# New durations in the planner that orders an attention stage, on one core

## The chip, the cores and the metric

The kernel runs on one core of a Trainium2 chip. The metric is the device time of one execution in microseconds; the time before is 968.0, the median of three runs (967.85 to 968.37). The engines are TensorE (PE for its matmuls, PEld for its weight loads), VectorE (DVE), ScalarE (ACT), GpSimd (POOL) and SyncE (SP, which only issues DMAs here). TensorE writes into PSUM, eight banks of 128 x 512 floats; the other engines read the banks, and a bank can take its next matmul only after its reader is done.

## The reference

For x of 2048 rows and 448 columns the kernel computes a gated mix of two branches, all in float32:

```python
g = sigmoid((x * gate_w).sum(-1, keepdims=True))
qkv = x @ wqkv                        # 16 heads of 28
scores = q @ k.T * 28 ** -0.5         # per head, 2048 x 2048
a = (softmax(scores) @ v) @ wo
b = (gelu(x @ w_gate) * (x @ w_up)) @ w_down    # 1792 hidden columns
out = g * a + (1 - g) * b
```

## The kernel before, in words

It has three stages. The first computes q, k and v from x. The last, behind attention, multiplies the hidden activations with w_down and the attention's output with wo. The middle one is attention, and TensorE's free slots in it are filled with the products x @ w_up and x @ w_gate. The change touches only the order of this middle stage.

Precision: each float32 operand is split into a high and a low part, so that a score tile takes three matmuls of a group (`product`), and a block of the hidden layer 42 (`cross`).

TensorE's array is used as four groups of 32 rows. A score needs only 28 rows plus two for a shift, and x and the weights of the hidden layer are laid out in pieces of 32 rows. So four matmuls, one for each row group, run side by side. The code calls this a step. In each step every group r does one matmul: either one of the three of its current score (`("score", ...)`, line 174), or one of its current hidden block (`("cross", ...)`, line 183). A group that has neither, or has no bank for a new block, has an empty slot in that step.

Attention goes in 32 turns: 16 heads, and for each head two halves of its keys (8 key tiles of 128 by 4 query tiles of 512: 32 score tiles). At a turn's end the value matmuls (`values`, 64 of them over the full array) sum the turn's exponentials into one bank, and DVE takes it out (`add`).

A score tile leaves its bank in one of two ways. Either ACT takes the exponential straight from the bank into SBUF (`exponential`, line 780), or DVE copies it to SBUF (`aside`, line 784) and ACT takes the exponential in place later. A finished hidden block is copied out by DVE (`clear`, line 797) and stored by SP. The eight banks serve all of this: up to four hidden blocks in progress, up to two scores in progress, and what waits for its reader.

The order of it all is written out before the kernel is built, by the function `plan` (lines 75 to 286). It is a small clockwork with its own time `s.now` for TensorE, `s.act`, `s.dve` and `s.sp` for the other queues, `s.bank[b]` for the moment at which bank b may be used again, and `s.tiles` for the exponentials' buffers. The constants at the top of the file are its durations in nanoseconds:

- STEP, the time of a step; READ and SEEN, from a score's end to the moment at which ACT and DVE may begin with it;
- EXP, what an exponential occupies ACT for, EXP_OUT, its time until the result is out; COPY, what a copy occupies DVE for and, before the change, also its time until the result is out;
- BACK, from a reader's end to the bank's next use;
- VALUES, INTO, OUTOF, the value matmuls of one key tile, the passage into them and out of them;
- ISSUE and LAND, SP's time for a DMA and a DMA's time to land.

`run` starts a score in some group as soon as a bank is free by this clock, at most two at a time. `step` advances all groups, and starts a new hidden block only when a bank is free. `end_score` decides between exponential and copy by which would be out first. `values` waits by the clock until the turn's exponentials are done. For each turn 25 preferences among the groups are tried, and the four states that promise the earliest end are carried on; the best at the end gives the list of operations.

The kernel then issues exactly this list. On the chip no time of the planner counts any more: each instruction waits for its semaphores, in the order of its engine's queue. What the planner's clock does is to choose the order, the bank of each block, and which tiles are copied.

Of the kernel before, what the change touches and what calls it, by code (L numbers as in the profile page):

```python
# [37 lines left out]

TURN, LEAD, NPT, FIRST = 8, 4, 36, 4
OFFSET = (0, 6, 21, 27)  # L40
STEP, READ, SEEN = 227, 270, 200
ISSUE, LAND = 520, 5000
EXP, EXP_OUT, COPY, BACK = 480, 620, 690, 100
VALUES, INTO, OUTOF = 857, 90, 203
EARLY = 7
HOLES = (0, 1, 2, 3)
XLOADS = (6, 9, 11, 14, 16, 19, 21, 24)
# [2 lines left out]
SLIP, LATE, AHEAD = 200, 12, 6  # L50
# [8 lines left out]
def piece(n):  # L59

    return n // 21 * 2 + (n % 21 >= 12)
# [13 lines left out]
def plan(blocks):  # L75
# [10 lines left out]

    def begin():
        s = State()
        s.now = s.act = s.dve = s.sp = s.turn = 0
        s.pos, s.next, s.since = list(OFFSET), [0] * 4, [0] * 4  # L90
        s.bank, s.tiles, s.where, s.seen = [0] * 8, [-n for n in range(NPT)], {}, {}
        s.score, s.mine = [None] * 4, [None] * 4
        s.late, s.waiting, s.arrive, s.stores = [], [], [], []
        s.parted = s.loaded = 6
        s.fetch = None
        s.ops, s.past = [], None
        return s

    def take(s):
        b = s.bank.index(min(s.bank))  # L100
        s.bank[b] = NEVER
        return b

    def next_tile(s, key):
        holes = HOLES if turn_of[key] == len(turns) - 1 else ()
        return min((t, n) for n, t in enumerate(s.tiles) if n not in holes)

    def hold(s, key):
        t, n = next_tile(s, key)
        s.where[key], s.tiles[n] = n, NEVER  # L110
        return t

    def run_act(s, key, src, ready):
        if src is not None:
            ready = max(ready, hold(s, key))
        t = max(s.act, ready)
        s.act = t + EXP
        s.seen[key] = t + EXP_OUT + BACK
        s.ops.append(("exp", key, s.where[key], src))
        if src is not None:  # L120
            s.bank[src] = s.seen[key]

    def run_late(s, until):
        s.late.sort(key=lambda a: (turn_of[a[1]], a[0]))
        while s.late and max(s.act, s.late[0][0]) <= until:
            ready, key = s.late.pop(0)
            run_act(s, key, None, ready)

    def run_dve(s, ready):
        s.dve = max(s.dve, ready) + COPY  # L130
        return s.dve + BACK

    def end_score(s, r):
        key, b, _ = s.score[r]
        s.score[r] = None
        run_late(s, s.now + READ - SLIP)
        tile = next_tile(s, key)[0]
        if s.waiting or tile == NEVER:
            s.waiting.append((key, b, s.now + READ))
            return  # L140
        direct = max(s.act, s.now + READ, tile) + EXP_OUT
        copied = max(s.dve, s.now + SEEN, tile) + COPY
        if copied - (0 if turn_of[key] == s.turn else SLIP) < direct and len(s.late) < LATE:
            s.bank[b] = run_dve(s, max(s.now + SEEN, hold(s, key)))
            s.ops.append(("copy", key, s.where[key], b))
            s.late.append((s.bank[b], key))
        else:
            run_act(s, key, b, s.now + READ)

    def fetch(s):  # L150
        if s.fetch is not None:
            run_sp(s, s.now, (5 if s.fetch % 2 else 8) if s.fetch < len(turns) - 2 else 0)
            s.ops.append(("fetch", s.fetch))
            s.fetch = None

    def run_sp(s, ready, n):
        s.sp = max(s.sp, ready) + ISSUE * n

    def store(s, until):
        while s.stores and s.stores[0][0] <= until:  # L160
            ready, *what = s.stores.pop(0)
            run_sp(s, ready, 1)
            s.ops.append(("store", *what))

    def can_cross(s, r):
        return s.pos[r] < end and piece(s.pos[r]) < s.parted

    def step(s):
        did = []
        for r in range(4):  # L170
            if s.score[r]:
                key, b, n = s.score[r]
                s.ops.append(("score", r, key, n, b))
                s.score[r][2] += 1
                did.append((r, True))
            elif can_cross(s, r) and (s.mine[r] is not None or min(s.bank) <= s.now):
                first = s.mine[r] is None
                if first:
                    s.mine[r] = take(s)
                n = s.pos[r]  # L180
                s.pos[r] += 1
                s.ops.append(("cross", r, n, s.mine[r], first, (n + 1) % 42 == 0 or n + 1 == goal[r]))
                did.append((r, False))
        s.now += STEP
        for r, scored in did:
            n = s.pos[r]
            if scored and s.score[r][2] == 3:
                end_score(s, r)
            if not scored and n < end and (n % 42 == 0 or n == goal[r]):
                b, s.mine[r] = s.mine[r], None  # L190
                s.bank[b] = run_dve(s, s.now + SEEN)
                s.ops.append(("clear", r, n - 1, b))
                s.stores.append((s.bank[b], r, n - 1))
                if n == goal[r]:
                    s.pos[r] = last
        while s.loaded < 2 * blocks + 8 and piece(min(s.pos)) >= s.loaded - 5:
            s.ops.append(("load", s.loaded))
            s.loaded += 1
            run_sp(s, s.now, 4)
            s.arrive.append(s.sp + LAND)  # L200
            fetch(s)
        store(s, s.now)
        while s.arrive and s.arrive[0] <= s.now:
            s.arrive.pop(0)
            s.parted += 1

    def run(s, n, todo, first, liking):
        want = sum(todo)
        done = k = 0
        while k < n or any(todo) or any(s.score):  # L210
            while done < want and k >= first and min(s.bank) <= s.now and sum(map(bool, s.score)) < 2:
                can = [r for r in range(4) if todo[r] and not s.score[r]]
                if not can:
                    break
                r = max(can, key=lambda r: (s.mine[r] is None, not 0 < -s.pos[r] % 42 <= 2, todo[r] + liking[r],
                                            s.now - s.since[r]))
                need = sum(not s.score[q] and (can_cross(s, q) if s.mine[q] is None else 0 < -s.pos[q] % 42 <= 2)
                           for q in range(4))
                if s.mine[r] is not None and (sum(b <= s.now for b in s.bank) <= need or done * n >= want * (k + AHEAD)):
                    break  # L220
                s.since[r] = s.now
                s.score[r] = [items[r][s.next[r]], take(s), 0]
                s.next[r] += 1
                todo[r] -= 1
                done += 1
            step(s)
            k += 1

    def values(s, i):
        store(s, NEVER)  # L230
        fetch(s)
        h, k0 = turns[i]
        keys = [(kt, (h, kt, q)) for kt in range(k0, k0 + TURN) for q in range(4)]
        while any(turn_of[key] == i for _, key in s.late):
            ready, key = s.late.pop(0)
            run_act(s, key, None, ready)
        s.now = max(s.now, min(s.bank), *(s.seen.pop(key) - VALUES * (kt - k0) for kt, key in keys))
        b = take(s)
        s.now += INTO
        s.ops.append(("values", i, b))  # L240
        for kt, key in keys:
            s.tiles[s.where.pop(key)] = s.now + VALUES * (kt - k0 + 1) + BACK
        while s.waiting:
            run_act(s, *s.waiting.pop(0))
        s.now += TURN * VALUES
        run_late(s, s.now + OUTOF)
        s.bank[b] = run_dve(s, s.now + SEEN) if i < len(turns) - 1 else NEVER
        s.now += OUTOF
        s.ops.append(("sum", i))

    def left(s):
        return sum(end - p if p >= last else g - p + 42 for g, p in zip(goal, s.pos))

    best = [begin()]
    for i, _ in enumerate(turns):
        tried = {}
        for old in best:
            for liking in [(0,) * 4, *permutations(range(4))]:
                for cut in CUTS if i == len(turns) - 1 else (0,):
                    s = old.copy()  # L260
# [15 lines left out]
    for s in best:  # L276
        while min(s.pos) < end:
            step(s)
        store(s, NEVER)
    s = min(best, key=lambda s: s.now)  # L280
    kept, free = s.mine, sorted((t, b) for b, t in enumerate(s.bank) if b not in s.mine)
    ops = []
    while s:
        ops = s.ops + ops
        s = s.past
# [778 lines left out]
```

## Time and profile before

| what | us |
|---|---|
| median of three runs | 968.0 |
| profiled execution | 967.61 |
| its span, first to last instruction | 965.8 |
| TensorE busy with matmuls | 959.8 |
| ACT busy | 658.3 |
| DVE busy | 564.4 |
| POOL busy | 416.1 |

In the views below a row of a group gives line, engine, operation, output<-input, shape and count, then busy time, mean duration in ns, and the idle time of that engine before it with what ended it. A row of one tile's view gives the durations as minimum, median and maximum in ns, and where in the span the first and the last lie. A row of the timeline gives the start and the duration in us; where several instructions are merged (x2, x3) the duration is from the first's start to the last's end. A row of windows gives the stretch, its length, TensorE's busy time with the count of its matmuls, the granted clock, the DMA share and GB/s. `b<-Q,wk` is a score's matmul, `b<-X,wk` one of the hidden layer, `b<-pt,VH` a value matmul, `pt<-b` an exponential or a copy out of a bank, `pt<-pt` an exponential in place, `u<-b` a hidden block's copy.

### The profile page before, as it was taken

What the parts mean: (1) busy time and instruction counts of PE and PEld (TensorE: products, weight loads), DVE (VectorE), ACT (ScalarE), POOL (GpSimd) and SP (SyncE); (2) the same over time, 40 slices, a digit from 0 to 9 for tenths busy, and PEclk for the clock granted to TensorE, in tenths of its full rate; (3) what the DMA queues carried; (4) which work ended last, traced back from release to release, by engine and by line L of the source; (5) the groups of instructions that cost most, each with busy time, mean ns of one, the idle gap of its engine ahead of it and who ended that gap; (6) DMA issues with size and microseconds to landing.
All of it is one profiled execution on the core that took longest, in us unless ns stands there. A gap on an engine that the chain in (4) does not pass through costs nothing.

```text
span 965.8 us, 27893 instructions
## 1 busy us (share of the span) xinstructions
PE 959.8 (99%) x11192; PEld 737.8 (76%) x11192; DVE 564.4 (58%) x873; ACT 658.3 (68%) x1260; POOL 416.1 (43%) x614
## 2 busy tenths in 40 slices
PE   9999999999999999999999999999999999999998
PEld 7878977666777776677777666777766679999997
DVE  6572366555656655566566555666655578765743
ACT  4332588776888778777788877788887797553530
POOL 6426553464646546554545655563564111210000
PEclk9999999999999999999999999999999999999999
DMA  7687786766667777666767775665776949967612
GB/s 237 205 269 225 249 223 169 216 182 181 189 192 194 203 190 197 177 172 194 196 176 217 209 204 147 202 183 170 216 197 186 288 138 343 328 215 250 202 60 77
DMA packets 108376, 194.83 MB, mean 202 GB/s; under 512 B 30716, under 2 KB 46108, under 8 KB 108244
## 3 DMA queue, kind: packets, MB, share of 16 engines
q1 hardware_dynamic: 92548, 160.98, 55.8%
q0 software_dynamic: 14864, 31.26, 11.3%
q8 instruction: 88, 1.44, 0.7%
q10 hardware_dynamic: 832, 0.79, 0.3%
q14 instruction: 44, 0.36, 0.1%
HBM read 131.99 MB, written 60.95 MB: 200 GB/s over the span
## 4 chain that ended last, share of the span: by engine, by line
PE 94%; DMA 3%; POOL 2%; issue 1%; SPq 0%; ACT 0%; DVE 0%; DVEq 0%; POOLq 0%; ACTq 0%
PE b L296 86%; PE pqk L296 7%; DMA vd<-V 1%; POOL wsd L302 1%; DMA VH<-vd 0%; DMA raw<-in_xT 0%; POOL whl L306 0%; DMA wsd<-whl 0%; DMA wraw<-in_wu 0%; DMA wk<-wsd 0%; POOL wk L302 0%; POOL whl L305 0%; SPq L299 0%; POOL wk L306 0%; POOL wk L305 0%
## 5 line engine op out<-in xcount | busy, mean ns | idle before, releaser
L296 PE MATMUL b<-X,wk 32*128 32x512 f32 x4704 | 459.9, 387 | 0.0
L296 PE MATMUL b<-Q,wk 32*128 32x512 f32 x3072 | 445.5, 390 | 0.0
L296 PEld LDWEIGHTS b<-X,wk 32*128 32x128 f32 x4704 | 407.2, 183 | 18.0 <-issue 12.0
L780 ACT ACTIVATE pt<-b 128x512 f32<-128x512 f32 x563 | 312.6, 601 | 140.8 <-PE b L296 134.9
L296 PEld LDWEIGHTS b<-Q,wk 32*128 32x128 f32 x3072 | 361.0, 183 | 27.7 <-issue 15.6
L784 DVE COPY pt<-b 128x512 f32<-128x512 f32 x461 | 309.8, 690 | 91.2 <-PE b L296 81.5
L780 ACT ACTIVATE pt<-pt 128x512 f32<-128x512 f32 x461 | 265.2, 627 | 0.0
L296 PE MATMUL b<-pt,VH 128*32 128x512 f32 x2048 | 226.4, 594 | 0.2 <-DMA VH<-vd 0.2
L296 PEld LDWEIGHTS b<-pt,VH 128*32 128x32 f32 x2048 | 63.8, 110 | 145.0 <-issue 134.8
L296 PE MATMUL b<-W,hl 128*128 128x448 f32 x648 | 129.9, 362 | 0.0
L296 PEld LDWEIGHTS b<-W,hl 128*128 128x128 f32 x648 | 121.5, 187 | 8.1
L309 ACT ACTIVATE hl<-hu 128x512 fp32r<-128x512 f32 x53 | 33.4, 629 | 62.2 <-PE b L296 56.0
L797 DVE COPY u<-b 128x512 f32<-128x512 f32 x108 | 73.6, 684 | 2.6 <-PE b L296 2.2
L826 DVE COPY o<-b 128x512 f32<-128x512 f32 x16 | 11.1, 692 | 105.5 <-issue 80.2
L828 DVE TENSOR_TENSOR o<-b,o 128x512 f32<-128x512 f32 x16 | 11.1, 691 | 102.2 <-PE b L296 102.2
L296 PE MATMUL pqk<-X,WQK 128*128 128x512 f32 (+1 forms) x308 | 69.3, 396 | 0.5 <-ACT X L309 0.5
L296 PEld LDWEIGHTS pqk<-X,WQK 128*128 128x128 f32 (+1 forms) x308 | 54.7, 189 | 15.3 <-issue 2.5
L302 POOL DMA_DIRECT2D wsd<-whl x112 | 58.9, 533 | 11.1 <-POOL whl L306 8.2
L302 POOL DMA_DIRECT2D rb<-rdend x64 | 31.7, 501 | 52.8 <-DMA rdend<-r 50.0
L306 DVE TENSOR_TENSOR hl<-hu,hl 128x512 fp32r<-128x512 f32 x53 | 36.5, 690 | 26.3 <-ACT hl L309 26.3
L306 POOL TENSOR_TENSOR wk<-kraw,wk 128x256 fp32r<-128x256 f32 x64 | 47.0, 735 | 5.2
L714 POOL TENSOR_TENSOR o<-o,rb 128x512 f32<-128x512 f32 x16 | 20.6, 1288 | 60.8 <-DMA rb<-rdend 60.8
(90 smaller groups left out, 657.2 us busy)
## 6 DMA issues: line engine op xcount, KB each, us to landing
wk<-wsd SPq DMA_DIRECT2D x228, 128.0 KB
ud<-u SPq DMA_DIRECT2D x111, 256.0 KB
wk<-wsd SPq DMA_DIRECT2D x228, 96.0 KB
hu<-ud SPq DMA_DIRECT2D x53, 256.0 KB
hg<-ud SPq DMA_DIRECT2D x49, 256.0 KB
qkd<-q SPq DMA_DIRECT2D x28, 256.0 KB
qraw<-qkd SPq DMA_DIRECT2D x64, 112.0 KB
wsd<-whl POOLq DMA_DIRECT2D x56, 128.0 KB, 3.2
```

The source lines that it names most:

```text
L296: return pin(nc.tensor.matmul(o, lhsT, rhs, start=start, stop=stop))
L302: return pin(nc.gpsimd.dma_start(out=out, in_=in_))
L306: pin(sub(lo, src, hi.bitcast(F32), OP.subtract))
L309: return nc.scalar.activation(o, i, AF.Copy)
L714: pin(nc.gpsimd.tensor_tensor(o, o, rb, OP.mult))
L780: pin(nc.scalar.activation(PT[key], PT[key] if b is None else sc[b], AF.Exp, scale=SCALE))
L784: pin(nc.vector.tensor_copy(PT[key], sc[b]))
L797: pin(nc.vector.tensor_copy(u, ps[b]))
L826: pin(nc.vector.tensor_copy(sums["o"], po))
L828: pin(nc.vector.tensor_tensor(sums["o"], po, sums["o"], OP.add))
```

## The change

Only the planner changes. READ goes from 270 to 200. EXP goes from 480 to 500. A copy now occupies DVE for 600 (COPY) and is out after 690 (COPY_OUT); before, 690 stood for both. BACK goes from 100 to 60. A bank counts as free 30 ns (SOON) before its time when a score or a hidden block is begun. OUTOF goes from 203 to 144, and the first step behind each turn's values takes 113 (START) longer. The kernel's own functions are the same; they get another list.

```diff
--- before.py
+++ after.py
@@ -38,10 +38,10 @@
 
 TURN, LEAD, NPT, FIRST = 8, 4, 36, 4
 OFFSET = (0, 6, 21, 27)
-STEP, READ, SEEN = 227, 270, 200
+STEP, START, READ, SEEN = 227, 113, 200, 200
 ISSUE, LAND = 520, 5000
-EXP, EXP_OUT, COPY, BACK = 480, 620, 690, 100
-VALUES, INTO, OUTOF = 857, 90, 203
+EXP, EXP_OUT, COPY, COPY_OUT, BACK, SOON = 500, 620, 600, 690, 60, 30
+VALUES, INTO, OUTOF = 857, 90, 144
 EARLY = 7
 HOLES = (0, 1, 2, 3)
 XLOADS = (6, 9, 11, 14, 16, 19, 21, 24)
@@ -86,7 +86,7 @@
 
     def begin():
         s = State()
-        s.now = s.act = s.dve = s.sp = s.turn = 0
+        s.now = s.act = s.dve = s.sp = s.turn = s.exit = 0
         s.pos, s.next, s.since = list(OFFSET), [0] * 4, [0] * 4
         s.bank, s.tiles, s.where, s.seen = [0] * 8, [-n for n in range(NPT)], {}, {}
         s.score, s.mine = [None] * 4, [None] * 4
@@ -127,8 +127,9 @@
             run_act(s, key, None, ready)
 
     def run_dve(s, ready):
-        s.dve = max(s.dve, ready) + COPY
-        return s.dve + BACK
+        t = max(s.dve, ready)
+        s.dve = t + COPY
+        return t + COPY_OUT + BACK
 
     def end_score(s, r):
         key, b, _ = s.score[r]
@@ -139,7 +140,7 @@
             s.waiting.append((key, b, s.now + READ))
             return
         direct = max(s.act, s.now + READ, tile) + EXP_OUT
-        copied = max(s.dve, s.now + SEEN, tile) + COPY
+        copied = max(s.dve, s.now + SEEN, tile) + COPY_OUT
         if copied - (0 if turn_of[key] == s.turn else SLIP) < direct and len(s.late) < LATE:
             s.bank[b] = run_dve(s, max(s.now + SEEN, hold(s, key)))
             s.ops.append(("copy", key, s.where[key], b))
@@ -173,7 +174,7 @@
                 s.ops.append(("score", r, key, n, b))
                 s.score[r][2] += 1
                 did.append((r, True))
-            elif can_cross(s, r) and (s.mine[r] is not None or min(s.bank) <= s.now):
+            elif can_cross(s, r) and (s.mine[r] is not None or min(s.bank) <= s.now + SOON):
                 first = s.mine[r] is None
                 if first:
                     s.mine[r] = take(s)
@@ -181,7 +182,8 @@
                 s.pos[r] += 1
                 s.ops.append(("cross", r, n, s.mine[r], first, (n + 1) % 42 == 0 or n + 1 == goal[r]))
                 did.append((r, False))
-        s.now += STEP
+        s.now += STEP + s.exit
+        s.exit = 0
         for r, scored in did:
             n = s.pos[r]
             if scored and s.score[r][2] == 3:
@@ -208,7 +210,7 @@
         want = sum(todo)
         done = k = 0
         while k < n or any(todo) or any(s.score):
-            while done < want and k >= first and min(s.bank) <= s.now and sum(map(bool, s.score)) < 2:
+            while done < want and k >= first and min(s.bank) <= s.now + SOON and sum(map(bool, s.score)) < 2:
                 can = [r for r in range(4) if todo[r] and not s.score[r]]
                 if not can:
                     break
@@ -216,7 +218,7 @@
                                             s.now - s.since[r]))
                 need = sum(not s.score[q] and (can_cross(s, q) if s.mine[q] is None else 0 < -s.pos[q] % 42 <= 2)
                            for q in range(4))
-                if s.mine[r] is not None and (sum(b <= s.now for b in s.bank) <= need or done * n >= want * (k + AHEAD)):
+                if s.mine[r] is not None and (sum(b <= s.now + SOON for b in s.bank) <= need or done * n >= want * (k + AHEAD)):
                     break
                 s.since[r] = s.now
                 s.score[r] = [items[r][s.next[r]], take(s), 0]
@@ -246,6 +248,7 @@
         run_late(s, s.now + OUTOF)
         s.bank[b] = run_dve(s, s.now + SEEN) if i < len(turns) - 1 else NEVER
         s.now += OUTOF
+        s.exit = START
         s.ops.append(("sum", i))
 
     def left(s):
```

## The prediction

> **What bounds the kernel now.** I read the page first, then the chain of waits, then the attention stage by windows and groups, and last single steps in the timeline.
>
> ```profile
> span 965.8 us, 27893 instructions
> PE 959.8 (99%) x11192; PEld 737.8 (76%) x11192; DVE 564.4 (58%) x873; ACT 658.3 (68%) x1260; POOL 416.1 (43%) x614
> 126.90 835.02 PE b L296 x10052
> 110.38:771.06 660.68, 660.51 (x9526) 1.00 0.69 196
> ```
>
> TensorE works without a hole from 126.90 for 835 us; the profiled execution took 967.61 us (span 965.8 plus 1.8 around it), 0.4 under the median of 968.0. The last row is the stretch from the first step of turn 0 to the first step of turn 31: 31 of the 32 turns, 660.68 us at full clock. The change reorders only this stage and a few microseconds of turn 31. What comes behind is bound by its own matmuls and stays.
>
> So the only question is how tightly the order packs TensorE. The groups of that window, then the whole-run spread of the durations:
>
> ```profile
> L296 PE MATMUL b<-X,wk 32*128 32x512 f32 x4553 | 445.1, 387 | 0.0
> L296 PE MATMUL b<-Q,wk 32*128 32x512 f32 x2988 | 432.9, 390 | 0.0
> L296 PEld LDWEIGHTS b<-Q,wk 32*128 32x128 f32 x2988 | 350.8, 183 | 27.1 <-issue 15.6 <-DVE pt L784 0.7 <-ACT pt L780 0.6
> ...
> L296 PE MATMUL b<-X,wk x4704: 382/383/499, 110.4 to 792.4; 32*128 32x512 f32 x196
> L296 PE MATMUL b<-Q,wk x3072: 382/383/499, 111.4 to 783.3; 32*128 32x512 f32 x192
> ```
>
> 4553 + 2988 = 7541 matmuls of a row group, four to a step: 1885 full steps. The pace of a step, the first step of a turn, and the passage through the value matmuls:
>
> ```profile
> 338.00 0.38 PE L296 MATMUL b<-Q,wk 32*128 32x512 f32 x1
> ...
> 338.91 0.38 PE L296 MATMUL b<-Q,wk 32*128 32x512 f32 x1
> 147.80 0.40 PE L296 MATMUL b<-X,wk 32*128 32x512 f32 x3
> 148.13 0.64 PE L296 MATMUL b<-pt,VH 128*32 128x512 f32 x4
> 155.13 0.50 PE L296 MATMUL b<-Q,wk 32*128 32x512 f32 x1
> 155.47 0.39 PE L296 MATMUL b<-Q,wk 32*128 32x512 f32 x1
> ```
>
> Four steps lie between the first two rows: 0.91/4 = 0.2275 us each. From the last step of a turn to the first of the next are 155.13 - 147.80 = 7.33, and that first step lasts 0.34, not 0.2275, with matmuls of 0.50 instead of 0.38: its weights are loaded late. Without any loss 31 turns take 1885 x 0.2275 + 31 x (7.33 + 0.34 - 2 x 0.2275) = 428.8 + 223.7 = 652.5. The stage loses 8.2 us of 660.7, and no better order can win more. It divides so: matmuls lengthened by late weights, ((387 - 383) x 4553 + (390 - 383) x 2988)/4 groups = 9.8, less 31 first steps at 0.113 (3.5), is 6.3. The rest is slots in which a row group had nothing to do; laying the order beside the trace I count 63 empty ones, 63 x 0.2275/4 = 3.6 (the two overlap by some of the skew between groups).
>
> **The change, part by part.** No instruction is added or removed, except that a tile may go by copy and second exponential instead of straight; only the planner's clock differs, and with it the order. So I ask of each constant: is it nearer to the trace, and what margin did the old one leave?
>
> ```profile
> 338.80 0.65 ACT L780 ACTIVATE pt<-pt 128x512 f32<-128x512 f32 x1
> 339.33 0.61 ACT L780 ACTIVATE pt<-b 128x512 f32<-128x512 f32 x1
> 334.82 1.09 ACT L780 ACTIVATE pt<-b 128x512 f32<-128x512 f32 x2
> 361.53 3.74 ACT L780 ACTIVATE pt<-pt 128x512 f32<-128x512 f32 x7
> 359.63 1.28 DVE L784 COPY pt<-b 128x512 f32<-128x512 f32 x2
> L780 ACT ACTIVATE pt<-b x563: 586/599/663, 112.3 to 783.7; 128x512 f32<-128x512 f32 x188
> L784 DVE COPY pt<-b x461: 680/692/695, 112.3 to 782.9; 128x512 f32<-128x512 f32 x154
> L797 DVE COPY u<-b x108: 680/682/694, 115.5 to 757.7; 128x512 f32<-128x512 f32 x108
> ```
>
> READ: the score matmul of 338.91 is read from 339.33; a step's end is its start plus 0.2275, so 193 ns later: 200 is right, 270 was 77 too many. EXP: two straight exponentials need 1.09 - 0.60 = 0.49 from start to start, seven from SBUF (3.74 - 0.62)/6 = 0.52: 500 is nearer than 480. COPY: 1.28 - 0.69 = 0.59: 600 is right, 690 was a copy's length, not its pace. START and OUTOF: 0.34 - 0.2275 = 113 is right. Where the old clock lagged TensorE at each turn by some 70 ns, the new one lags by about 20. As a clock the new planner is better throughout.
>
> A sentence of the Trainium skill speaks against COPY = 600: VectorE: DVE Perf Modes, section "The DRAIN you can't avoid", says that the next VectorE instruction starts only once the pipe is empty. By it a copy queued behind another would free its bank 90 ns later than planned; the row of 359.63, two copies in 1.28, shows the overlap, so here the measurement decides and I carry it as a small rival.
>
> BACK is the constant that I doubt. It says how long after its reader's end a bank's next matmul may start without loss: 100 before, 60 less SOON's 30 now. The trace has two looks at it:
>
> ```profile
> 463.76 0.69 DVE L784 COPY pt<-b 128x512 f32<-128x512 f32 x1 [0.55 <-PE b L296]
> 464.51 0.18 PEld L296 LDWEIGHTS b<-Q,wk 32*128 32x128 f32 x1 [0.37 <-DVE pt L784]
> 464.51 0.50 PE L296 MATMUL b<-X,wk 32*128 32x512 f32 x2
> 464.85 0.39 PE L296 MATMUL b<-X,wk 32*128 32x512 f32 x2
> ...
> 541.21 0.69 DVE L784 COPY pt<-b 128x512 f32<-128x512 f32 x1 [0.36 <-PE b L296]
> 541.96 0.18 PEld L296 LDWEIGHTS b<-Q,wk 32*128 32x128 f32 x2 [0.18 <-DVE pt L784]
> 542.01 0.44 PE L296 MATMUL b<-Q,wk 32*128 32x512 f32 x1
> 542.29 0.39 PE L296 MATMUL b<-Q,wk 32*128 32x512 f32 x2
> ```
>
> The wait hangs on the weight load, not on the matmul. In the first case the copy ends at 464.45, the load starts 0.06 later, all four matmuls behind it are 0.50 long, and the next step comes 0.34 later: 113 ns lost beyond the wait. In the second the matmul starts 0.11 after the copy's end (541.90) and needs 0.44, and the next step comes after 0.28: 50 to 60 lost. So a reuse is free of cost only from about 55 + 113 = 165 ns behind the reader's end; below that it costs 165 less the gap, and 113 plus the wait where the load stands still. BACK = 60 is the reaction of a load that was already late. Behind the waiting load stand the loads of the other groups, as the rows of 464.51 show.
>
> On this the Trainium skill (TensorE: Matmul & The Clock Gate, section "The mechanism") says that a weight load for another row group is pulled ahead of matmuls in flight; if that held past a load that waits, one group of four would be late, and my loss below would shrink to about a quarter. At 464.51 the four started together, so I don't count on it.
>
> Now the margins, for the tightest reuse each planner allows. Straight exponential, really free 193 + 599 = 792 ns after its step's end: before 270 + 620 + 100 = 990, a gap of 198, no loss; after 200 + 620 + 60 - 30 = 850, a gap of 58, late by 107. Copy, really free at 193 + 692 = 885: before 990, gap 105, late by 60; after 920, gap 35, a load that waits. Reuses happen on the grid of steps. An exponential that finds ACT idle: before five steps (1135, gap 343), after 880 fits into four (908, gap 116, late by 49). A copy that finds DVE idle: five steps both times (gap 250), no loss. One queued behind others ends anywhere on the grid: average lateness of an exponential (165 - 58)²/(2 x 227) = 25, of a copy or clear (165 - 35)²/(2 x 227) = 37.
>
> How many: of 563 straight exponentials 184 start over 0.56 behind ACT's start before (ACT idle), 379 are queued; of 461 + 108 DVE evictions about 320 find DVE idle, 250 are queued. All taken at once: 184 x 49 + 379 x 25 + 250 x 37 = 27.7 us of lateness. Not all are: of the 1131 pairs of a reader and the next user of its bank in the trace, 750 lie within 0.425, i.e. bound by the bank; groups 1 to 3 start up to 0.05 after group 0, which takes some 20 from each; and a late TensorE gives a queued ACT and DVE time to catch up. Bounds: 6.3 (as now; the better clock pays for the thinner margin) and 28 (all). I take 0.4 of it, 11, and 2 of today's that no constant touches (weights, K): 13, 6.7 more than now.
>
> Against it stand the empty slots. Up to the whole 3.6 could be filled, since a bank counts as free 70 to 140 ns earlier; some 20 of the 63 wait for the end of the weights or of the list, so I take 2.4, between 0 and 3.6. SP's queue and the weight loads keep their places in the list to a step or two. Loads for two turns ahead hide that; nothing of them is counted.
>
> Sum in the profiled execution: 967.6 + 6.7 - 2.4 = 971.9; beside the median of 968.0, about 972.
>
> **The rivals.**
> Faster: the truer clock wins. With EXP = 500 the planner no longer believes in banks that a loaded ACT hasn't freed, and the limit of two scores in flight, not the bank, paces most reuses, so gaps stay. For it: all constants but BACK agree with the trace. Against it: 750 of 1131 reuses are within 0.425. Empty slots -2.4, lateness 0 to -2: -3, 965. It decides if lateness stays under 6.3 + 2.4.
> No change: lateness up by as much as the slots give, 2.4: 968. It also covers an order that hardly differs.
> Much slower: every reuse at the first moment allowed, 0.7 of 27.7 = 19 plus 2, less 6.3, less 2.4: +12.7, 981. Against it: queued evictions catch up.
> VectorE's pace is 690 after all: 250 queued evictions, each 90 later, bound by the bank in 750 of 1131 and half of it hidden: +7.5 on top, 980. The row of 359.63 speaks against it; 0.02.
>
> **How the numbers follow.** A measurement of this kernel tells 0.2% (1.9 us) from no change. Chances: forecast, slower by 2 to 9 us, 0.36; much slower 0.09; pace of 690 0.02; no change 0.18; faster 0.35, since four constants of five move towards the trace and only one away from what it shows. So slower 0.47, same 0.18, faster 0.35. The forecast's own range is 970 to 977. The range for 8 in 10 holds the faster case with all empty slots filled and 0.9 of lateness gained (968.0 - 3.6 - 0.9 = 963.5), and reaches up to the heavy one: 963.5 to 981.
>
> **What would show it.** Right: mean duration of the two matmul groups up from 387 and 390 by 3 to 4 ns (6.7 x 4/7776), the score loads' idle time on ACT and DVE up from 1.3 us to 4 or more, and many matmuls of 0.40 to 0.50 inside turns. Empty slots under 40. The stretch of 31 turns over 663. Wrong: those means at 387 and 390 or below while the stretch shrinks under 659, which would mean that banks weren't what paced the reuses; or a stretch unchanged with other tiles copied. If more than 500 tiles are copied, ACT's second passes (0.52 against 0.49) could make the value matmuls wait: 7.33 would grow.

## The result, and the profile after

The changed kernel takes 979.28 us (median of six runs) against 968.18 on the same chips: 1.17% slower, interval 1.0100 to 1.0134, so about 11.3 us. The direction was forecast and the time lies inside the range, near its upper end; the forecast itself was 972, a change of 4 instead of 11.

The page, the chain of waits and the stretch from turn 0's first step to turn 31's, then from there to the last stage's first matmul; the last two rows are the same stretches before.

```profile
span 977.4 us, 27862 instructions
PE 971.4 (99%) x11192; PEld 728.2 (74%) x11192; DVE 558.9 (57%) x863; ACT 683.3 (70%) x1260; POOL 417.5 (43%) x614
127.74 845.81 PE b L299 x9817
110.50:781.15 670.65, 670.30 (x9508) 1.00 0.67 192
781.15:804.34 23.19, 23.19 (x321) 1.00 0.46 126
```

```profile
110.38:771.06 660.68, 660.51 (x9526) 1.00 0.69 196
771.06:792.72 21.66, 21.66 (x303) 1.00 0.39 108
```

TensorE still works without a hole at full clock, and the span is 11.6 us longer: 10.0 in the 31 turns, 1.5 in the last turn, 0.1 outside. Over the whole run it does the same matmuls, only more slowly; 18 of the attention stage's (7541 less 7523, 4.5 steps or 1.0 us) have moved from the 31 turns into the last one, which is most of the 1.5 there. The groups of the 31 turns after the change:

```profile
L299 PE MATMUL b<-X,wk 32*128 32x512 f32 x4535 | 455.2, 390 | 0.0
L299 PE MATMUL b<-Q,wk 32*128 32x512 f32 x2988 | 428.7, 395 | 0.0
L299 PEld LDWEIGHTS b<-X,wk 32*128 32x128 f32 x4535 | 382.1, 183 | 30.4 <-issue 17.9 <-ACT pt L783 2.5
L299 PEld LDWEIGHTS b<-Q,wk 32*128 32x128 f32 x2988 | 329.8, 183 | 34.3 <-issue 9.6 <-ACT pt L783 6.2 <-DVE o L829 2.5
```

Means rose from 387 and 390 ns to 390 and 395, and the weight loads of the scores, which had waited 0.6 us for ACT, wait 6.2. By the sum used in the prediction, the 7523 matmuls of these turns need 651.6 us without any loss (1880.75 steps of 0.2275 plus 223.7), so the loss is 19.1 instead of 8.2. Summed matmul by matmul beyond 383 ns, divided by the four groups and less the 3.5 us of the 31 first steps, the lengthening is 14.2 us, before 6.9. Empty slots fell from 63 to 29 (3.6 to 1.7 us). The rest, what is left of the loss beside these two terms, went from -2.4 (the terms overlap) to 3.3; steps that began late because a load stood still are part of it.

One such place, in the timeline. A score's last matmul starts at 422.30, so its step ends at 422.53; four steps later, at 423.44, the order has another score in the same bank.

```profile
422.30 0.39 PE L299 MATMUL b<-Q,wk 32*128 32x512 f32 x2
422.07 1.25 ACT L783 ACTIVATE pt<-b 128x512 f32<-128x512 f32 x2
423.37 0.18 PEld L299 LDWEIGHTS b<-Q,wk 32*128 32x128 f32 x1 [0.18 <-ACT pt L783]
423.37 0.18 PEld L299 LDWEIGHTS b<-X,wk 32*128 32x128 f32 x2
423.38 0.28 PEld L299 LDWEIGHTS b<-Q,wk 32*128 32x128 f32 x2
423.37 0.50 PE L299 MATMUL b<-X,wk 32*128 32x512 f32 x2
423.71 0.40 PE L299 MATMUL b<-X,wk 32*128 32x512 f32 x3
```

The second of the two exponentials ends at 422.07 + 1.25 = 423.32. The load that needs its bank starts 0.05 later, the loads behind it start with it, the matmuls need 0.50 for 0.38, and the next step comes after 0.34. The loads of the other row groups did not pass the one that waited, here as before the change. The Trainium skill (TensorE: Matmul & The Clock Gate, section "The mechanism") has such loads pulled ahead of matmuls in flight; at this place none got past the load that waits for its semaphore, four loads standing between 423.37 and 423.38. Over the whole trace, the pairs of an ACT reader's end and the next matmul in its bank that lie closer than 0.165 us grew from 46 of 544 to 146 of 551; for DVE from 53 of 587 to 85 of 580. (The pairs take the n-th matmul by start for the n-th of the list. Within a step the row groups do not always start in the list's order, so a single gap can be off by their skew; with scores and hidden matmuls counted each in its own order the two ACT counts are 54 and 146, and the counts of the table below come out up to 15 higher.)

Which exponentials these are can be read from ACT's order. A straight exponential that starts more than 0.56 us behind the start before it, as in the prediction, found ACT idle; the others were queued. Of the changed kernel's 146 close pairs 116 stand behind an exponential that found ACT idle and 30 behind a queued one; before, 4 and 42.

### The profile page after: what moved, and what is told of

Read it like the earlier page. It is cut to its first block, busy times and chain, and to the rows that moved or that the text cites. A ratio compares the mean times of both kernels' runs of the same rounds, so it can differ in the third digit from the quotient of the medians.

```text
span 977.4 us, 27862 instructions
## 1 busy us (share of the span) xinstructions
PE 971.4 (99%) x11192; PEld 728.2 (74%) x11192; DVE 558.9 (57%) x863; ACT 683.3 (70%) x1260; POOL 417.5 (43%) x614
## 4 chain that ended last, share of the span: by engine, by line
PE 94%; DMA 4%; POOL 1%; issue 1%; SPq 0%; ACT 0%; DVE 0%; DVEq 0%; POOLq 0%; ACTq 0%
PE b L299 87%; PE pqk L299 7%; DMA vd<-V 1%; DMA kraw<-qkd 1%; DMA VH<-vd 1%; DMA wsd<-whl 0%; DMA raw<-in_xT 0%; DMA wraw<-in_wu 0%; POOL wsd L305 0%; POOL whl L309 0%; DMA wk<-wsd 0%; SPq L302 0%; POOL wk L309 0%; POOL whl L308 0%; POOL wk L305 0%
## 5 line engine op out<-in xcount | busy, mean ns | idle before, releaser
L299 PE MATMUL b<-X,wk 32*128 32x512 f32 x4704 | 471.5, 391 | 0.0
L299 PE MATMUL b<-Q,wk 32*128 32x512 f32 x3072 | 440.9, 395 | 0.0
L783 ACT ACTIVATE pt<-b 128x512 f32<-128x512 f32 x573 | 330.0, 599 | 127.3 <-PE b L299 109.5
L299 PEld LDWEIGHTS b<-X,wk 32*128 32x128 f32 x4704 | 395.1, 183 | 31.8 <-issue 18.7
L299 PEld LDWEIGHTS b<-Q,wk 32*128 32x128 f32 x3072 | 339.7, 183 | 36.0 <-issue 10.6
L787 DVE COPY pt<-b 128x512 f32<-128x512 f32 x451 | 305.7, 690 | 92.5 <-PE b L299 80.5
L783 ACT ACTIVATE pt<-pt 128x512 f32<-128x512 f32 x451 | 248.1, 623 | 0.0
```

Of the source, the lines that this page charges most:

```text
L299: return pin(nc.tensor.matmul(o, lhsT, rhs, start=start, stop=stop))
L783: pin(nc.scalar.activation(PT[key], PT[key] if b is None else sc[b], AF.Exp, scale=SCALE))
L787: pin(nc.vector.tensor_copy(PT[key], sc[b]))
```

## The experiments

All kernels are the changed one with other constants; each is compared with the kernel before on its own chip. Two theories stood at the start. The first: the margins did it (READ, BACK and SOON let a bank be used again before its weight load can come in time). The second: the paces did it (EXP, COPY and the turn's times make the planner give the readers other work). The column "late" is the lengthening of the matmuls in the 31 turns, counted as above; the last two columns count the close pairs.

| kernel | median us | ratio to before, interval | late us | ACT pairs under 0.165 us | DVE pairs under 0.165 us |
|---|---|---|---|---|---|
| before | 968.2 to 968.4 | | 6.9 | 46 of 544 | 53 of 587 |
| changed | 979.28 | 1.0117 (1.0100 to 1.0134) | 14.2 | 146 of 551 | 85 of 580 |
| margins only | 978.97 | 1.0109 (1.0092 to 1.0126) | 14.4 | 212 of 610 | 44 of 521 |
| paces only | 969.5 | 1.0019 (1.0005 to 1.0033) | 6.5 | 19 of 523 | 63 of 608 |
| changed, BACK 165, SOON 0 | 967.85 | 0.9997 (0.9986 to 1.0008) | 5.8 | 19 of 565 | 64 of 566 |
| changed, SOON 0 | 976.96 | 1.0089 (1.0072 to 1.0105) | 12.7 | 153 of 567 | 80 of 564 |
| changed, SOON 0, BACK 88 | 976.67 | 1.0071 (1.0048 to 1.0094) | 13.6 | 160 of 559 | 89 of 572 |
| changed, SOON 0, BACK 89 | 972.14 | 1.0030 (1.0017 to 1.0044) | 7.9 | 29 of 583 | 92 of 548 |
| changed, SOON 0, BACK 100 | 969.04 | 1.0007 (0.9992 to 1.0022) | 5.8 | 16 of 575 | 64 of 556 |
| changed, SOON 0, READ 229 | 968.58 | 1.0005 (0.9990 to 1.0021) | 7.1 | 21 of 521 | 88 of 610 |
| before, READ 200 | 971.81 | 1.0034 (1.0024 to 1.0044) | 6.8 | 43 of 587 | 51 of 544 |
| before, BACK 60 | 971.59 | 1.0028 (1.0013 to 1.0043) | 7.2 | 58 of 545 | 67 of 586 |
| before, SOON 30 | 968.18 | 0.9993 (0.9981 to 1.0005) | 7.0 | 46 of 544 | 67 of 587 |
| changed, SOON 0, BACK 140, 16 states | 968.35 | 0.9994 (0.9981 to 1.0007) | 5.4 | 14 of 569 | 63 of 562 |

The column "late" follows the sum of the two counts, whichever engine the pairs are behind. Over these 14 kernels a straight line of 1.9 us plus 0.048 us for each close pair meets it within 1.1 us, and a fit with separate slopes gives 0.049 for ACT's pairs and 0.046 for DVE's, the latter with an error of 0.009. So by these runs a close pair goes with the same lengthening behind either reader; what differs is how many of them a planner's constants make.

### Margins or paces

The first kernel has the changed margins on the old paces, the second the changed paces on the old margins.

```diff
-STEP, START, READ, SEEN = 227, 113, 200, 200
-EXP, EXP_OUT, COPY, COPY_OUT, BACK, SOON = 500, 620, 600, 690, 60, 30
-VALUES, INTO, OUTOF = 857, 90, 144
+STEP, START, READ, SEEN = 227, 0, 200, 200
+EXP, EXP_OUT, COPY, COPY_OUT, BACK, SOON = 480, 620, 690, 690, 60, 30
+VALUES, INTO, OUTOF = 857, 90, 203
```

> READ 200, BACK 60 and SOON 30 as in the changed kernel; EXP 480, COPY 690 for pace and length, OUTOF 203 and no longer first step as before. Theory (thin margins: weight loads of reused banks come late): nearly the whole loss is here, +6 to +12 us against before, with the means of the score and hidden matmuls up to 394 and 390 ns. Rival (the new paces of ACT and DVE overbook the readers, or the turn's clock is worse): this kernel stays within 2 us of before.

```diff
-STEP, START, READ, SEEN = 227, 113, 200, 200
-EXP, EXP_OUT, COPY, COPY_OUT, BACK, SOON = 500, 620, 600, 690, 60, 30
+STEP, START, READ, SEEN = 227, 113, 270, 200
+EXP, EXP_OUT, COPY, COPY_OUT, BACK, SOON = 500, 620, 600, 690, 100, 0
```

> EXP 500, COPY 600 with COPY_OUT 690, OUTOF 144 and START 113 as in the changed kernel; READ 270, BACK 100 and SOON 0 as before. Theory: -2 to +2 us against before, mean durations of 387 and 390 ns or less. Rival (the paces do it): +8 to +12 us.

The margins alone give +10.6 us (1.0109), the whole loss within the intervals. The paces alone give +1.8 us (1.0019), about what can just be told from no change. Whole-run groups of the two:

```profile
L299 PE MATMUL b<-X,wk 32*128 32x512 f32 x4704 | 470.2, 390 | 0.3 <-DMA wk<-wsd 0.3
L299 PE MATMUL b<-Q,wk 32*128 32x512 f32 x3072 | 447.0, 396 | 0.0
```

```profile
L299 PE MATMUL b<-X,wk 32*128 32x512 f32 x4704 | 459.5, 387 | 0.9 <-DMA wk<-wsd 0.9
L299 PE MATMUL b<-Q,wk 32*128 32x512 f32 x3072 | 436.2, 390 | 0.0
```

With the margins the means are 390 and 396, with the paces 387 and 390 as before. The second theory falls. Of the 212 close ACT pairs of the margins alone, 102 are behind exponentials that found ACT idle and 110 behind queued ones, against 116 and 30 in the changed kernel. The paces go with far fewer of the queued ones, and yet the time is the same. The theory also falls in the other direction: true paces on the old margins gained nothing.

### Giving the margin back

```diff
-EXP, EXP_OUT, COPY, COPY_OUT, BACK, SOON = 500, 620, 600, 690, 60, 30
+EXP, EXP_OUT, COPY, COPY_OUT, BACK, SOON = 500, 620, 600, 690, 165, 0
```

> The changed kernel with BACK 165 and SOON 0: a bank counts as free only when its weight load comes in time (the 55 plus 113 ns of the trace of before). Theory: the loss is gone, -3 to +1 us against before, mean matmul durations under 387 and 390. Rival (true clock is not enough, the paces overbook, or banks are now short): +5 us or more, or more than 100 empty slots.

```diff
-EXP, EXP_OUT, COPY, COPY_OUT, BACK, SOON = 500, 620, 600, 690, 60, 30
+EXP, EXP_OUT, COPY, COPY_OUT, BACK, SOON = 500, 620, 600, 690, 60, 0
```

> The changed kernel with SOON 0 alone. Theory: a reuse may still come 165 - 88 = 77 ns late, the loads that stand still become few: about a quarter of the loss comes back, +7 to +10 us against before (changed kernel +11). Rival (SOON alone does it): within 2 us of before. Rival (paces): as the changed kernel, +11.

BACK 165, the prediction's own figure for a load that comes in time, takes the whole loss away (0.9997). It does not win: late loads fell only from 6.9 to 5.8, and 68 slots are empty, about as many as before (63). SOON alone is worth 2 to 3 us of the loss; DVE pairs under 0.06 us fall from 40 to 13 without it, ACT's only from 49 to 40. Of the 40, 23 stand behind the copy at a turn's end (`add`); without SOON none does.

### One nanosecond: the grid of steps

An exponential that finds ACT idle frees its bank, by the planner, READ + EXP_OUT + BACK after its step. Four steps are 908. So the theory of the grid says that the loss is not spread over margins but jumps where this sum passes 908.

```diff
-EXP, EXP_OUT, COPY, COPY_OUT, BACK, SOON = 500, 620, 600, 690, 60, 30
+EXP, EXP_OUT, COPY, COPY_OUT, BACK, SOON = 500, 620, 600, 690, 88, 0
```

> The changed kernel with SOON 0 and BACK 88. Theory (the grid of steps): an exponential read from an idle ACT frees its bank, by the planner, 200 + 620 + 88 = 908 ns after its step's end, exactly four steps of 227; so the order still reuses it after four steps, really 116 ns behind the reader, 49 late: +4 to +7 us against before. Rival (only the size of the margin counts, smoothly): BACK 88 and 89 cost the same, within 1 us.

```diff
-EXP, EXP_OUT, COPY, COPY_OUT, BACK, SOON = 500, 620, 600, 690, 60, 30
+EXP, EXP_OUT, COPY, COPY_OUT, BACK, SOON = 500, 620, 600, 690, 89, 0
```

> The same with BACK 89: 909 ns, which no longer fits into four steps; the bank is used again after five (1135, a real gap of 343). Theory: 0 to +3 us against before, at least 2 us under the kernel with BACK 88, though a single nanosecond differs. Rival: the same as BACK 88.

```diff
-EXP, EXP_OUT, COPY, COPY_OUT, BACK, SOON = 500, 620, 600, 690, 60, 30
+EXP, EXP_OUT, COPY, COPY_OUT, BACK, SOON = 500, 620, 600, 690, 100, 0
```

> The same with BACK 100 (SOON 0, READ 200): by the size of the margin alone (100 + 28 = 128 ns behind an exponential's end, 100 + 5 behind a copy's, both under 165) this should still cost +3 us or more. By the grid the four-step reuse is gone and only queued readers come late, some 20 ns on average: -1 to +2 us against before.

Between 88 and 89 lie 4.5 us (976.67 and 972.14 on the same chip), between intervals that don't touch, while the 28 ns from BACK 60 (the kernel with SOON 0, 1.0089) to 88 (1.0071) change nothing that can be told. The stretches of the 31 turns differ by 4.5 us too, so it is not the end of the list; these stretches and the groups of the two, 88 first:

```profile
110.17:780.05 669.88, 667.41 (x9511) 1.00 0.67 193
110.30:775.64 665.34, 661.73 (x9522) 1.00 0.68 195
```

```profile
L299 PE MATMUL b<-X,wk 32*128 32x512 f32 x4704 | 468.3, 390 | 0.1
L299 PE MATMUL b<-Q,wk 32*128 32x512 f32 x3072 | 443.9, 395 | 0.0
L299 PEld LDWEIGHTS b<-Q,wk 32*128 32x128 f32 x3072 | 348.0, 183 | 31.4 <-issue 9.9 <-ACT pt L783 5.9 <-DVE u L800 0.8
```

```profile
L299 PE MATMUL b<-X,wk 32*128 32x512 f32 x4704 | 461.3, 388 | 1.3 <-DVE u L798 1.3
L299 PE MATMUL b<-Q,wk 32*128 32x512 f32 x3072 | 441.4, 391 | 0.2 <-DVE u L798 0.2
L299 PEld LDWEIGHTS b<-Q,wk 32*128 32x128 f32 x3072 | 359.3, 183 | 25.7 <-issue 15.2 <-DVE u L800 0.7 <-DVE u L798 0.7
```

The score loads' wait for ACT, 5.9 us, is gone from the list of 89, and the ACT pairs under 0.165 us go from 160 to 29: those behind an exponential that found ACT idle from 153 to 16, those behind a queued one from 7 to 13. Of the exponentials that found ACT idle, a quarter had their bank used again within 0.114 us at 88, the 116 ns of the prediction; at 89 that quartile is 0.284. BACK 100 is back at the time before, although its margin by size alone is still under 165.

The 3.7 us that BACK 89 still costs over before are not late loads (7.9 against 6.9). In its profile the values of turn 0 wait 2.1 us for V, as those of the kernel with BACK 100 do for 1.6 (before 0.2), and 70 slots are empty instead of 63. TensorE also stands idle 1.6 us for a hidden block's copy-out (`u`, L798, in the rows above), which in the chain of waits comes behind the DMAs `wk<-ud` and `ud<-u`. These two waits are 3.5 us more than before in the one execution that was profiled. Whether they make the 3.7 us is not shown: the profile with BACK 88 has a wait of 2.3 us in turn 0 as well, for ACT.

### Which reader carries it

```diff
-STEP, START, READ, SEEN = 227, 113, 200, 200
-EXP, EXP_OUT, COPY, COPY_OUT, BACK, SOON = 500, 620, 600, 690, 60, 30
+STEP, START, READ, SEEN = 227, 113, 229, 200
+EXP, EXP_OUT, COPY, COPY_OUT, BACK, SOON = 500, 620, 600, 690, 60, 0
```

> The changed kernel with SOON 0 and READ 229: 229 + 620 + 60 = 909 ns, one over four steps, while copies and hidden blocks keep BACK 60. Theory (straight exponentials at four steps carry most of the loss): 0 to +4 us against before, at least 3 us under the kernel with SOON 0 and READ 200 (+8.7). Rival (copies and clears with BACK 60 carry it): +6 us or more.

Here only the straight exponential is moved over four steps (909); copies and hidden blocks keep BACK 60. The time is back at that before (1.0005), 8 us under the same kernel with READ 200. DVE's pairs under 0.165 us are 88 of 610 and under 0.06 us 22, more than before (53 of 587 and 5), and still nothing is lost: the stretch of 31 turns is that of before. ACT's pairs fell from 46 to 21 at the same time, so that all close pairs together are 109, against 99 before and 231 in the changed kernel.

```profile
110.31:770.51 660.20, 659.96 (x9509) 1.00 0.67 195
```

So the straight exponentials at four steps carry the loss. BACK 60 on DVE's banks makes only some 35 close pairs more, about 1.7 us at 0.048 each, and the ACT pairs that went pay for most of it.

### Each margin alone, on the old paces

The edits are written against the kernel before. The files that ran are the changed one with the old constants (START 0, COPY_OUT 690, OUTOF 203), by which its planner keeps the same clock.

```diff
-STEP, READ, SEEN = 227, 270, 200
+STEP, READ, SEEN = 227, 200, 200
```

> The kernel before with READ 200 alone (BACK 100, SOON 0, all paces old). The planner frees a bank behind an idle ACT after 200 + 620 + 100 = 920 ns, over four steps (908). Theory by the grid alone: -1 to +2 us against before, as with BACK 100 and the new paces (+0.7). Rival (thin margin hurts together with the old EXP of 480, 20 to 40 ns short per queued exponential): +3 us or more.

```diff
-EXP, EXP_OUT, COPY, BACK = 480, 620, 690, 100
+EXP, EXP_OUT, COPY, BACK = 480, 620, 690, 60
```

> The kernel before with BACK 60 alone: 270 + 620 + 60 = 950 ns behind an idle ACT, over four steps as well; copies 950 too. Grid alone: -1 to +2 us. Rival (thin margin with the old paces): +3 us or more, and the more of it with copies, whose gap shrinks to 65.

The third is the kernel before with SOON 30 in the three lines that use it.

> The kernel before with SOON 30 alone: 990 - 30 = 960 ns for both readers, over four steps. Grid: -1 to +2 us. Thin margin: +1 to +3 us, since 30 ns are less than READ's 70 or BACK's 40.

None of the three passes under 908 for an idle ACT (920, 950, 960), and late loads stay at 6.8 to 7.2. Yet the first two cost 3.3 and 2.7 us, more than the -1 to +2 that the grid alone gave. My rival called it thin margins with an EXP that is too short; the trace of READ 200 says otherwise. Its two stretches:

```profile
110.38:770.69 660.31, 659.87 (x9507) 1.00 0.66 195
770.69:796.14 25.45, 25.45 (x323) 1.00 0.58 164
```

The 31 turns are as fast as before (660.31 against 660.68, with 19 matmuls or 1.1 us less in them); the last turn, which has those, takes 25.45 instead of 21.66. In its list 75 matmuls of hidden blocks are left behind the last value matmuls, before 22, and in many of its steps two of the four groups have nothing left: 62 empty slots in turn 31 instead of 13. So the loss lies in how the search ended the list; the late loads are those of before (6.8 and 6.9). The changed kernel with SOON 0 has the same (65 left, 58 empty slots, 25.26 us), so its 8.7 us hold 3.6 of that, and its stretch of 31 turns, 666.23, shows what the margin cost there:

```profile
110.26:776.49 666.23, 665.79 (x9508) 1.00 0.66 193
776.49:801.75 25.26, 25.26 (x322) 1.00 0.59 152
```

With BACK 60 alone (its profile is of the slowest of ten executions, 975.1 us at a granted clock of 0.996) 1.9 us of turn 0 wait for V, the last turn is 2.0 longer (39 empty slots), and 81 slots are empty in the 31 turns; which of the three makes its loss I have not separated, so this one stays open.

### A better version

```diff
-EXP, EXP_OUT, COPY, COPY_OUT, BACK, SOON = 500, 620, 600, 690, 60, 30
+EXP, EXP_OUT, COPY, COPY_OUT, BACK, SOON = 500, 620, 600, 690, 140, 0
-KEPT, CUTS = 4, (0, 10, 20, 40, 60)
+KEPT, CUTS = 16, (0, 10, 20, 40, 60)
```

> The changed kernel with SOON 0, BACK 140 and 16 states carried from turn to turn instead of 4. A try for a version that beats both: -2 to 0 us against before if the search was what was left, since empty slots and late loads each still cost some microseconds; as the kernel with BACK 165 (967.85) if not.

It has the shortest stretch of 31 turns of all profiles and the fewest late loads:

```profile
110.43:769.46 659.03, 658.16 (x9523) 1.00 0.68 196
```

But 0.9994 (0.9981 to 1.0007) is no difference that can be measured. It beats the changed kernel by 11 us and the one before by nothing that I can show.

## Why the prediction was right, and where its size was off

Against the terms of its sum, the 11.6 us of the profiled span are: longer matmuls 7.3 (forecast 6.7), empty slots -1.9 (-2.4), the other loss of the 31 turns 5.6 (no term), the last turn without the matmuls that moved into it 0.5 (no term).

- What bounds the stage, and that no order could win more than some 8 us: nothing here speaks against it. No kernel here won a measurable part of it.
- BACK 60 takes the reaction of a load that is already late for the time of one that costs nothing; the free gap is 165 ns: right. BACK 165 took the loss away, but so did BACK 100, by the grid; the 165 itself rests on the durations: in the trace of before matmuls at gaps of 0.09 to 0.105 us have a median near 0.45 us, from 0.165 us on 0.388 and less.
- The grid: right, and stronger than I used it. An exponential that found ACT idle was to come back after four steps with 116 ns; it did (quartile 114 at BACK 88), and one nanosecond more took 4 us away.
- The term that was mis-sized is the count. "184 start over 0.56 behind ACT's start before" was taken from the old order and kept; in the new order 390 of the straight exponentials whose bank has a next user find ACT idle, against 179 in the old. I then gave all classes the same 0.4, and the largest part of the 27.7 us to queued exponentials and copies. Of the 132 close pairs that the change added, 112 are behind exponentials that found ACT idle; behind queued ones there are 12 fewer, behind DVE 32 more. The late loads lengthened by 7.3 us, near the 6.7 of the sum, by two errors that cancelled.
- The step that failed is that lateness shows only in longer matmuls. The loss grew by some 5.6 us (3.3 and the -2.4 of before) beside the lengthening and the empty slots. With SOON a load also stands still, and then the step itself begins late: pairs under 0.06 us rose from 11 to 89, and the steps within two of such a reuse, by the mean start of their groups, are 9.2 us slower than before, 6.6 of it longer matmuls and 2.5 later starts. The other 3 us are not placed. The prediction priced such a case ("113 plus the wait where the load stands still") but put none into the sum.
- Empty slots: -2.4 forecast, -1.9 measured (63 to 29). The signs named in advance came: means up by 3 to 5 ns (3 to 4 were named), waits for ACT and DVE of 4 us and more, under 40 empty slots, a stretch over 663.
- "What comes behind stays" held for the last stage, but not for the last turn: 1.5 us there were in no term, 1.0 of them matmuls that the 31 turns no longer do, and in the experiments this turn is up to 3.8 us longer than before.
- The faster rival fell: its condition, lateness under 8.7, was missed at 14.2. The rival of VectorE's pace fell too: COPY 600 with COPY_OUT 690 in the kernel with READ 229 costs nothing.

## What to carry to other kernels

A wait that is measured where an engine was already waiting is its reaction time, not the notice it needs; take the notice from the shortest gap at which the instruction behind it has its normal length. On a grid of equal steps a planner's constant acts through where its sums cross the grid, so ask which sum crosses before sizing a margin, and test one unit on both sides. A truer clock in a planner is no gain by itself: the old errors were also the slack that kept weight loads ahead.

## What the runs showed that I had not expected

- One nanosecond in one constant moved the kernel by 4.5 us (BACK 88 and 89), with the rest of the file unchanged.
- A bank that is used again under 0.165 us behind its reader costs about 0.048 us of longer matmuls on average, behind ACT and behind DVE alike, and this line holds over 14 orders. The 88 DVE pairs of the kernel with READ 229 cost nothing beside before, where ACT had 25 pairs more.
- The last turn of a searched order varies by up to 3.8 us (21.66 to 25.45). In the longest about 1.1 us is matmuls that moved there from the turns ahead, and 2.8 are 49 more empty slots. I find no constant that it follows.
